# Moving SyncE's DMA transposes behind the output stores, and one spread from GpSimd's queue to SyncE's, in a fused attention and GEGLU kernel

## The chip, the cores and the metric

The kernel runs on one core of a Trainium2 chip. The metric is the device time in microseconds (us), the median of several executions. A second number, the span of a profiled execution, goes from the first to the last instruction of the program in that execution.

Engines are named as the profile names them: PE (TensorE, matmuls; PEld is its weight load), DVE (VectorE), ACT (ScalarE), POOL (GpSimd) and SP (SyncE). SP computes nothing here: it only waits for semaphores and issues DMAs, one after the other, so that an instruction which waits holds up all that stand behind it. A "q" behind an engine's name marks its sequencer.

## The reference

Sliding-window attention with an ALiBi bias over 8 batches of 8 heads, 576 positions and 64 dimensions, then a GEGLU feed-forward block over the 4608 tokens:

```
rel = pos[:, None] - pos[None, :]
mask = (rel >= 0) & (rel < 128)
scores = where(mask, q @ k.T / sqrt(D) + slopes * -abs(rel), -1e9)
attn = softmax(scores) @ v                      # 8 batches, 8 heads, 576 x 64
x = attn.transpose(0, 2, 1, 3).reshape(4608, 512)
g, val = x @ w_gate, x @ w_val                  # 512 -> 1536
out = (gelu(g) * val) @ w_out                   # 1536 -> 512, float32
```

## The kernel before

The feed-forward part runs over nine groups of 512 tokens (`for g in range(NG)`, group 0 to 8). In each group PE first makes the 12 blocks of hidden features (`gate_val` for one block, `gate_quad` for four blocks with seven instead of eight block products), and then the output (`out_products`). Attention for a later batch is woven into the same groups. In groups 2 to 5, group g does this for batch b = g + 2: the scores of b (`scores2`, from the transposed queries `qT` and keys `kT`), the exponentials and the sums over windows (`add`); and for batch b - 1 = g + 1 the row sums (`sums4`), their inverses, the products with the values (`values`) and the scaling into `xT`.

The order on each engine is written by hand: instructions stand on an engine in the order in which the code names them, and semaphores hold each one until what it needs is there. For batches 3 to 7 the data take this way:

- **Loads** on POOL's queue (`load_qk`, `load_v`): at f == 6 of group g POOL issues the q and k rows of batch g + 3 into `qs`, `ks` and the v rows of batch g + 2 into `vb`, 15 DMAs. They follow POOL's own arithmetic of the group.
- **Transposes** on SP's queue (`transposes_dma`): five DMAs turn `qs` into `qT`, one turns `ks` into `kT`. Before the change they are called at the start of groups 1 to 5. For batches 5 to 7 (groups 3 to 5) k comes ahead of q.
- **Gather** on SP's queue (ACT's for batch 3): three small DMAs write the inverse row sums `r` of batch g + 1 to a buffer `rd` in DRAM, issued at f == 5 (for batches 3 and 7 between two steps of the quad at f == 6).
- **Spread** on SP's queue (POOL's for batch 3): two DMAs of 576 KB read `rd` back, each row repeated over 64 partitions, into `rb`, at f == 6. DVE multiplies the value products by `rb` (L554).
- **Stores** on SP's queue: finished output tiles `osb` are collected in a list and issued by `store()`, in the middle of `out_products` and at f == 1 of the next group. The last of a group's tiles is finished by DVE at L927.

In groups 3 to 5 SP's order is therefore: transposes of k, of q, the two stores left from the group before, gather, spread, and two stores in the middle of the products. The first transpose waits for the rows of k, and everything behind it waits with it.

Of the kernel before, what the change touches and what calls it, by code (L numbers as in the profile page):

```python
# [35 lines left out]
def kernel(  # L36
# [10 lines left out]
    nc = tc.nc  # L47
    B, H, S, D = q.shape
# [26 lines left out]
    def keep_busy(ps, n, w=64, rhs=None):  # L75
        for _ in range(n):
# [23 lines left out]
    qs, ks = ([consts.tile([128, 5, DM], BF16, name=f"{nm}s{i}") for i in range(2)]  # L100
              for nm in "qk")
    qT, kT = ([consts.tile([128, 4, 640], BF16, name=f"{nm}T{i}") for i in range(2)]
              for nm in "qk")
# [16 lines left out]
    def load_qk(b):  # L120
        load(qs[b % 2], q, b)
        load(ks[b % 2], k, b)

    def load_v(b, js=range(5)):
        load(vb[b % 2], v, b, js, 64)
# [48 lines left out]
        for n, lo in ((0, 0), (1, 384)):  # L174
            untangle(copy, b, n, what, c, c + 1, ps[:, lo:576])

    def transposes_dma(b):
        def of_k():
            nc.sync.dma_start_transpose(
                out=kT[b % 2].rearrange("p c (j t) -> p (c j) t", t=128),  # L180
                in_=ks[b % 2].rearrange("p j x -> p (j x)"))

        if b > 4:
            of_k()
        for j in range(5):
            nc.sync.dma_start_transpose(
                out=qT[b % 2][:, :, 128 * j:128 * j + 128], in_=qs[b % 2][:, j, :])
        if b <= 4:
            of_k()


    Ps = [consts.tile([128, H, 896], BF16, name=f"P{i}") for i in range(2)]
# [254 lines left out]

    def spread_dma(b):
        for i in (0, 1):
            (nc.gpsimd if b == 3 else nc.sync).dma_start(  # L450
                out=recip[b][64 * i:64 * i + 64, :, :],
                in_=flat[b][i:H:2, :].unsqueeze(0).to_broadcast((64, 4, S)))

# [214 lines left out]
    def store():  # L668
        for args in stores:
            nc.sync.dma_start(**args)  # L670
        stores.clear()
# [79 lines left out]
    def flat_of(t):  # L751
        return t.rearrange("p a x -> p (a x)")
# [10 lines left out]
    def combine_weights(f0, engine=nc.gpsimd):  # L763
        todo, to = [], sums_w[f0]
        for c in (0, 1):
            g1, g2, v1, v2 = (weights(w, x, f0) for w, x in ((wg, c), (wg, 2 + c), (wv, c), (wv, 2 + c)))
            s1, s2, s3, s4 = (cut(t[:, c, :], 2) for t in to)
            todo.append([lambda o=o, a=a, b=b, op=op: engine.tensor_tensor(out=o, in0=a, in1=b, op=op)
                         for o, a, b, op in ((s1, v1, v2, ALU.add), (s2, s1, g1, ALU.subtract),
                                              (s3, g1, v1, ALU.subtract), (s4, g2, s2, ALU.subtract))])  # L770
        return [do for pair in zip(*todo) for do in pair]
# [23 lines left out]
    def tiles_of(ts, lo=0):  # L795
        return [flat_of(t)[:, lo + 512 * i:lo + 512 * i + 512] for t, n in ts for i in range(n)]

    def wide_of(ts):
        return [cut(flat_of(t).bitcast(FP32)[:, 512 * i:512 * i + 512], 2) for t, n in ts for i in range(n)]
# [156 lines left out]
    for h in (0, 2, 4, 6):  # L956
        for w, src in ((0, q), (1, k)):
            (nc.scalar if w and h == 0 else nc.sync).dma_start(  # L958
                out=raw[w][h // 4].rearrange("p (h x) -> p h x", h=4)[:, h % 4:h % 4 + 2, :],
                in_=src[0][h:h + 2, 0:384, :].rearrange("h (p r) d -> p h (r d)", r=3))  # L960
# [114 lines left out]
    for do in inverse_a:  # L1075
        do[1]()
    dve(out=pairs1.rearrange("p x (h d) -> p h x d", d=64),
        in_=vb[1].rearrange("p j x -> p (j x)")[:, 0:1536].rearrange(
            "p (h x d) -> p h x d", h=H, x=3))
# [46 lines left out]
    for n in range(4):  # L1126
        nc.gpsimd.dma_start(
            out=wo[:, 3 * n:3 * n + 3, :],
            in_=moe_w_out[384 * n:384 * n + 384, :].rearrange("(c p) f -> p c f", p=128))
# [193 lines left out]
    put_off = {}  # L1323

    for g in range(NG):
        if 1 <= g < B - 2:
            transposes_dma(3 if g == 1 else g + 2)
        if g == NG - 1:
            nc.gpsimd.tensor_copy(out=mark, in_=flat_of(T)[0:1, 1536:1538])
            sums = combine_weights(4)  # L1330
            for do in sums[:6]:
                do()
            gate_quad(g, 0)
            store()
            for do in sums[6:]:
                do()
            gate_quad(g, 6)
            for lo, hi in ((0, 2), (3, 5)):
                combine_left(g, lo, hi, (0, 1), engine=nc.gpsimd)
            gate_quad(g, 4, (wide_of([(kT[1], 2), (vb[0], 2), (vb[1], 2)]), tiles_of([(qs[1], 4)])), high=nc.vector)  # L1340
            out_products(g)
            continue
        if g == B - 1:
            for f in range(NF):
                if f in QUADS:
                    gate_quad(g, f)
                elif not any(f0 < f < f0 + 4 for f0 in QUADS):
                    gate_val(g, f)
                if f == 4:
                    store()  # L1350
                if f == 5:
                    combine_left(g, 0, 2, (0, 1), engine=nc.gpsimd)
                if f == 6:
                    combine_left(g, 2, 3, (0, 1))
                    combine_left(g, 0, 2, (3, 2), engine=nc.gpsimd)
            for which in ((0, 1), (3,), (2,)):
                for lo, hi in ((3, 5), (5, 6)) if 0 in which else ((2, 5), (5, 6)):
                    combine_left(g, lo, hi, which)
            out_products(g)
            continue  # L1360
        if g == 1:
            room = rooms(1)
            sums = combine_weights(6, nc.vector)
            for do in sums[:5]:
                do()
        for f in range(9 if g == 0 else 0, NF):
            if f == 6 and g:
                gate_quad(g, 6, room if g == 1 else None,
                          (lambda: gather(g + 1)) if g in (2, B - 2) else None)
            elif not (g and 6 < f < 10):  # L1370
                gate_val(g, f)
            if g == 1:
                for do in {0: sums[5:7], 1: sums[7:]}.get(f, ()):
                    do()
                if f in (1, 2, 3):
                    combine_x(1, 0, 256, {1: (0,), 2: (1, 2), 3: (3,)}[f])
                if f in (4, 5, 10, 11):
                    combine_right({4: 0, 5: 1, 10: 2, 11: 3}[f])
            if f in put_off:
                put_off.pop(f)()  # L1380
            if f == 1:
                store()
            if g == 0 and f == 10:
                masks_of_last_blocks(0, 8)
            if g == 0 and f == 9:
                for c in range(4):
                    for w in (0, 1):
                        transpose(1, w, c, (act, dve)[w])
            if g < 2:
                continue  # L1390
            if g == 2 and f == 2:
                add(3, 2, act, (1,))
            if f == (0 if g == 2 else 3 if g == B - 2 else 2):
                nc.gpsimd.tensor_copy(out=mark, in_=hid[g][0:1, f, 510:512])  # L1394
                combine_x(g, engine=nc.gpsimd)
            if f == 3 and 2 < g < B - 2:
                combine_left(g, 0, 2, (0, 1, 3, 2), engine=nc.gpsimd)
            if f == (5 if g == 2 else 4):
                sums4(g + 1)
            if f == 5:  # L1400
                if 2 < g < B - 2:
                    combine_left(g, 2, 3, (0, 1), engine=nc.gpsimd)
                    gather(g + 1)
                else:
                    combine_left(g, 0, 3, (0, 1), engine=nc.gpsimd)
            if g == B - 2 and f == 2:
                combine_x(g + 1, 0, 192)
            if f == 6:
                spread_dma(g + 1)
            if f == 6:  # L1410
                if g + 3 < B:
                    load_qk(g + 3)
                if g + 2 < B:
                    load_v(g + 2)
            if f == 11:
                combine_left(g, 3, 6, (0, 1))
        if g == 1:
            nc.gpsimd.tensor_copy(out=mark, in_=kT[1][0:1, 0, 512:514])
            load_qk(4)
            load_v(3)  # L1420
        if g == 0:
            nc.gpsimd.memset(Ps[0][:, :, 0:64], 0.0)
            for t in (qs[1], ks[1]):
                nc.gpsimd.memset(t[64:128, 4, :], 0.0)
        if g in PRODUCTS:
            out_products(g)
        else:
            for item in steps(g):
                if isinstance(item, int):
                    out_part(g, item)  # L1430
                else:
                    RUN[item[0]](*item[1:])
            store()
        if g == 0:
            load_v(2)
            nc.gpsimd.tensor_copy(out=mark, in_=qT[0][0:1, 0, 512:514])
            load_qk(3)
# [30 lines left out]
```

## Time and profile before

| What | Value |
|---|---|
| Device time, median of 3 executions | 323.19 us (322.78 to 323.5) |
| The profiled execution's own time | 322.87 us |
| Span of that execution | 321.1 us (1.8 us lie around it) |
| Granted TensorE clock, mean | 1.000 |
| Instructions in the span | 9392 |
| Bytes moved by DMA | 43.57 MB, mean 136 GB/s |

The profiled execution is 0.32 us under the median. The page lists the busy time of each engine, the chain of work that ended last, the costliest groups of instructions and the DMA queues. DMA queue q0 carries what POOL issues, q1 what SP and ACT issue, and q8 is a queue of the kind "instruction". The timeline view lists an engine's instructions in order of time, with start and duration in us and, in brackets, the idle time ahead of a row and what ended it. The windows view gives, for a stretch of time, the busy time of each engine and in brackets the number of its instructions that lie in it. The DMA view lists, for a stretch, the packets, megabytes and share of the 16 DMA engines' time of each queue.

### The profile page before, as it was taken

The page shows a single profiled execution, that of the slowest core. Times are in us where ns is not written, and L with a number is a line of the kernel's source. Part 1 is how long each engine was busy: PE and PEld are TensorE (multiplying, and loading weights), DVE is VectorE, ACT ScalarE, POOL GpSimd, SP SyncE. Part 2 cuts the span into 40 slices and gives each one's busy share as a digit, 9 for nine tenths or more (in the row PEclk, how much of TensorE's full clock was granted, in tenths as well). Part 3 has the DMA queues.
Part 4 walks back from the last instruction along what each step waited for, and adds up shares of the span by engine and source line. Part 5 has one row for each costly group of instructions (what it writes and reads, how often), then busy time and mean ns, then how long its engine had stood idle before and what let it go on. Part 6 is the DMA issues. An engine that isn't in the chain of part 4 may idle for free.

```text
span 321.1 us, 9392 instructions
## 1 busy us (share of the span) xinstructions
PE 314.4 (98%) x3729; PEld 214.9 (67%) x3729; DVE 251.5 (78%) x493; ACT 222.3 (69%) x427; POOL 207.1 (65%) x239
## 2 busy tenths in 40 slices
PE   8999999999999999999999999999999999999995
PEld 3566746465554768476765786578747787788884
DVE  7789666979779887978698679877898856895883
ACT  7984678557888688757865787578767256627852
POOL 5974579384068977589856995496009496446750
PEclk9999999999999999999999999999999999999999
DMA  8999999999999959994999499949203330003003
GB/s 213 168 195 192 199 178 184 141 172 193 95 181 165 153 128 208 171 145 133 188 193 153 141 187 195 150 138 179 101 34 83 72 133 0 0 2 133 0 4 131
DMA packets 149724, 43.57 MB, mean 136 GB/s; under 512 B 133688, under 2 KB 143024, under 8 KB 149680
## 3 DMA queue, kind: packets, MB, share of 16 engines
q0 software_dynamic: 107744, 19.28, 76.6%
q1 hardware_dynamic: 41472, 23.35, 32.5%
q8 instruction: 29, 0.48, 0.6%
q10 hardware_dynamic: 464, 0.35, 0.3%
q14 instruction: 15, 0.12, 0.2%
HBM read 43.65 MB, written 9.53 MB: 166 GB/s over the span
## 4 chain that ended last, share of the span: by engine, by line
PE 94%; DMA 2%; DVE 1%; issue 1%; ACT 1%; SPq 1%; DVEq 0%
PE ps L644 35%; PE ps L837 21%; PE ps L748 21%; PE ps L495 6%; PE ps L680 4%; PE ps L306 2%; PE ps L700 2%; PE ps L220 2%; DMA ks<-in_k_dram 2%; PE ps L434 1%; PE ps L158 1%; SPq L958 1%; ACT P L235 0%; DVE xT L534 0%; ACT rb L597 0%
## 5 line engine op out<-in xcount | busy, mean ns | idle before, releaser
L644 PE MATMUL ps<-xT,wv 128*128 128x512 bf16 (+3 forms) x292 | 67.7, 353 | 0.0
L644 PE MATMUL ps<-xT,wg 128*128 128x512 bf16 (+3 forms) x292 | 67.6, 353 | 0.0
L650 ACT ACTIVATE gelu<-ps 128x512 bf16<-128x512 f32 (+3 forms) x73 | 39.3, 544 | 37.7 <-PE ps L644 33.9
L235 ACT ACTIVATE P<-ps 128x512 bf16<-128x512 f32 (+1 forms) x108 | 52.3, 578 | 5.2 <-PE ps L306 3.3
L651 DVE TENSOR_TENSOR hT<-ps,gelu 128x512 bf16<-128x512 f32 (+3 forms) x73 | 43.3, 619 | 15.3 <-PE ps L644 12.0
L644 PEld LDWEIGHTS <-wv 128*128 128x128 bf16 x292 | 27.5, 98 | 28.3 <-issue 0.2
L644 PEld LDWEIGHTS <-wg 128*128 128x128 bf16 x292 | 26.8, 98 | 25.2 <-issue 1.0
L116 POOL DMA_DIRECT2D vb<-in_v_dram x40 | 34.1, 880 | 6.9 <-DMA ks<-in_k_dram 2.0
L240 DVE TENSOR_TENSOR P<-P,emask 128x768 bf16<-128x768 bf16 x60 | 31.9, 554 | 7.6 <-ACT P L235 5.7
L748 PEld LDWEIGHTS <-hT 128*128 128x128 bf16 x336 | 32.0, 98 | 5.6
L116 POOL DMA_DIRECT2D ks<-in_k_dram x30 | 25.4, 887 | 3.3 <-DMA rb<-rd 2.0
L837 PEld LDWEIGHTS <-kept 128*128 128x128 bf16 x256 | 25.0, 98 | 3.0
L748 PEld LDWEIGHTS <-left 128*128 128x128 bf16 x252 | 24.2, 98 | 4.2 <-issue 0.9
L116 POOL DMA_DIRECT2D qs<-in_q_dram x30 | 25.4, 869 | 1.8 <-DMA wo<-in_moe_w_out_dram 1.0
L1394 POOL COPY mark<-hT 1x2 bf16<-1x2 bf16 x5 | 0.9, 174 | 35.1 <-DVE hT L651 35.1
L748 PE MATMUL ps<-right,hT 128*128 128x256 bf16 x168 | 22.2, 273 | 0.0
L845 DVE TENSOR_TENSOR qT<-ps,qT 128x512 f32<-128x512 f32 x20 | 12.9, 686 | 11.2 <-PE ps L837 9.8
L748 PE MATMUL ps<-right,left 128*128 128x256 bf16 x168 | 20.6, 273 | 0.8 <-issue 0.8
L748 PE MATMUL ps<-wo,hT 128*128 128x256 bf16 x168 | 21.2, 273 | 0.0
L837 PE MATMUL ps<-xT,wg 128*128 128x256 bf16 x176 | 21.0, 273 | 0.0
L845 DVE TENSOR_TENSOR P<-ps,P 128x512 f32<-128x512 f32 x24 | 15.0, 682 | 6.9 <-PE ps L837 6.9
L837 PEld LDWEIGHTS <-wg 128*128 128x128 bf16 x176 | 17.2, 98 | 3.4 <-issue 0.2
(179 smaller groups left out, 639.1 us busy)
## 6 DMA issues: line engine op xcount, KB each, us to landing
out_dram<-osb SPq DMA_DIRECT2D x34, 256.0 KB
rb<-rd SPq DMA_DIRECT2D x8, 576.0 KB
vb<-in_v_dram POOLq DMA_DIRECT2D x32, 128.0 KB, 6.8
qs<-in_q_dram POOLq DMA_DIRECT2D x24, 128.0 KB, 6.5
ks<-in_k_dram POOLq DMA_DIRECT2D x24, 128.0 KB, 7.8
wo<-in_moe_w_out_dram POOLq DMA_DIRECT2D x4, 384.0 KB, 12.1
wg<-in_moe_w_gate_dram POOLq DMA_DIRECT2D x5, 256.0 KB, 8.2
wv<-in_moe_w_val_dram POOLq DMA_DIRECT2D x5, 256.0 KB, 8.8
```

The source lines that it names most:

```text
L116: nc.gpsimd.dma_start(out=t[at:at + n, j, :].rearrange("p (h d) -> p h d", h=H), in_=src[b][:, 128 * j:128 * j + n, :].rearrange("h p d -> ...
L220: nc.tensor.matmul(out=out, lhsT=keys(b, c, m)[half, :], rhs=qT[b % 2][half, c, q0:q0 + n], start=first, stop=True, skip_group_check=not f ...
L235: nc.scalar.activation(out=dst, in_=src, func=AF.Exp, scale=0.125)
L240: nc.vector.tensor_tensor(out=dst, in0=dst, in1=m, op=ALU.mult)
L495: mm = nc.tensor.matmul(out=out, lhsT=lhsT, rhs=prob(b)[half, c, i, col:col + q1 - q0], start=all(t[2] != u for t in todo[:n]), stop=True, ...
L644: nc.tensor.matmul(out=ps, lhsT=w[:, c, 128 * f:128 * (f + 1)], rhs=xT[:, c, t0 + lo:t0 + hi], start=begins, stop=(c == 3), skip_group_che ...
L650: nc.scalar.activation(out=gl[:, 0:n], in_=pg, func=AF.Gelu)
L651: nc.vector.tensor_tensor(out=hid[g][:, f, lo:hi], in0=pv, in1=gl[:, 0:n], op=ALU.mult)
L680: nc.tensor.matmul(out=acc[g], lhsT=hid[g][:, f, 128 * t:128 * (t + 1)], rhs=wo[:, f, :], start=(f == 0), stop=(f == NF - 1))
L748: nc.tensor.matmul(out=made[g, a, into], lhsT=lhsT, rhs=rhs, start=first and k == 0, stop=count + k == NF // 2 - 1, skip_group_check=True)
L837: nc.tensor.matmul(out=ps[:, 256 * e:256 * e + 256], lhsT=lhsT, rhs=x[:, c, :], start=n in (1, 2, 5) and e == 0 and c == 0, stop=c == 1, s ...
L845: nc.vector.tensor_tensor(out=to[u], in0=cut(banks[n, u], to[u].shape[1]), in1=to[u], op=ALU.add)
```

## The change

The transposes of groups 1 and 2 stay where they were, at the start of the group. Those of groups 3 to 5 move to f == 1, behind `store()`, and q comes ahead of k in all of them. The spread of batch 3 is issued by SP instead of POOL.

```diff
-    def transposes_dma(b):
-        def of_k():
-            nc.sync.dma_start_transpose(
-                out=kT[b % 2].rearrange("p c (j t) -> p (c j) t", t=128),
-                in_=ks[b % 2].rearrange("p j x -> p (j x)"))
-
-        if b > 4:
-            of_k()
-        for j in range(5):
-            nc.sync.dma_start_transpose(
-                out=qT[b % 2][:, :, 128 * j:128 * j + 128], in_=qs[b % 2][:, j, :])
-        if b <= 4:
-            of_k()
+    def transposes_dma(b, what=range(6)):
+        for j in what:
+            if j == 5:
+                nc.sync.dma_start_transpose(
+                    out=kT[b % 2].rearrange("p c (j t) -> p (c j) t", t=128),
+                    in_=ks[b % 2].rearrange("p j x -> p (j x)"))
+            else:
+                nc.sync.dma_start_transpose(
+                    out=qT[b % 2][:, :, 128 * j:128 * j + 128], in_=qs[b % 2][:, j, :])
...
     def spread_dma(b):
         for i in (0, 1):
-            (nc.gpsimd if b == 3 else nc.sync).dma_start(
+            nc.sync.dma_start(
...
     for g in range(NG):
-        if 1 <= g < B - 2:
-            transposes_dma(3 if g == 1 else g + 2)
+        if 1 <= g < 3:
+            transposes_dma(g + 2)
...
             if f == 1:
                 store()
+                if 2 < g < B - 2:
+                    transposes_dma(g + 2)
...
             if f == 6:
                 spread_dma(g + 1)
-            if f == 6:
                 if g + 3 < B:
                     load_qk(g + 3)
```

SP's instructions from the transposes of group 2 to the middle of group 3, in the kernel before (numbers in the names are buffers; L670 stores, L186 and L179 transposes, L445 gather, L450 spread):

```order
L186 DMA_TRANSPOSE qT_99<-qs_95 128x4x128 x5
L179 DMA_TRANSPOSE kT_101<-ks_97 128x20x128
L670 DMA out_dram<-osb 128x512 x2
L179 DMA_TRANSPOSE kT_102<-ks_98 128x20x128
L186 DMA_TRANSPOSE qT_100<-qs_96 128x4x128 x5
L670 DMA out_dram<-osb 128x512 x2
L445 DMA rd<-r 8x192 x3
L450 DMA rb<-rd 64x4x576 x2
```

The same stretch in the changed kernel, whose lines are four fewer (L666 stores, L184 and L180 transposes, L441 gather, L446 spread):

```order
L184 DMA_TRANSPOSE qT_99<-qs_95 128x4x128 x5
L180 DMA_TRANSPOSE kT_101<-ks_97 128x20x128
L446 DMA rb<-rd 64x4x576 x2
L666 DMA out_dram<-osb 128x512 x4
L184 DMA_TRANSPOSE qT_100<-qs_96 128x4x128 x5
L180 DMA_TRANSPOSE kT_102<-ks_98 128x20x128
L441 DMA rd<-r 8x192 x3
L446 DMA rb<-rd 64x4x576 x2
```

The spread of batch 3 now stands behind the transposes of batch 4; the two stores of the middle of group 2 and the two left over stand together as four; q and k have changed places. In groups 4 and 5 the order changes in the same way. On POOL, the end of group 2 before the change:

```order
L721 TENSOR_TENSOR left<-left,hT 128x768
L892 TENSOR_TENSOR hT<-P_105,vb_103 128x2x256 x2
L450 DMA rb<-rd 64x4x576 x2
L116 DMA qs_96<-in_q_dram 128x8x64 x4
L116 DMA qs_96<-in_q_dram 64x8x64
L116 DMA ks_98<-in_k_dram 128x8x64 x4
```

and in the changed kernel:

```order
L717 TENSOR_TENSOR left<-left,hT 128x768
L888 TENSOR_TENSOR hT<-P_105,vb_103 128x2x256 x2
L116 DMA qs_96<-in_q_dram 128x8x64 x4
L116 DMA qs_96<-in_q_dram 64x8x64
L116 DMA ks_98<-in_k_dram 128x8x64 x4
```

The two DMAs of the spread are gone from POOL, and the loads of batch 5 follow its last multiplication directly. PE, DVE and ACT keep their instructions in the same order.

## The prediction

> **What bounds the kernel now.** I read the page first, then PE group by group, then its one gap.
>
> ```profile
> PE 314.4 (98%) x3729; PEld 214.9 (67%) x3729; DVE 251.5 (78%) x493; ACT 222.3 (69%) x427; POOL 207.1 (65%) x239
> PE 94%; DMA 2%; DVE 1%; issue 1%; ACT 1%; SPq 1%; DVEq 0%
> q8 instruction: 29, 0.48, 0.6%
> ```
>
> PE is busy for 98% of the span and makes 94% of the chain that ended last. SP and POOL, on which everything in this change stands, are nearly absent from the chain. So the change can only pay, or cost, where PE waits. The windows of groups 2, 3, 4 and 5, cut where PE begins each group's first gate product, show how much that is (columns: length, busy PE, PEld, DVE, ACT, POOL, clock, DMA share, GB/s):
>
> ```profile
> 95.67:128.96 33.29, 33.29 (x410) 22.99 (x405) 28.76 (x53) 26.74 (x48) 28.37 (x32) 1.00 1.60 166
> 128.96:163.16 34.20, 33.44 (x406) 23.04 (x404) 27.30 (x56) 24.82 (x43) 26.74 (x30) 1.00 1.40 165
> 163.16:196.44 33.28, 33.28 (x406) 23.04 (x404) 26.84 (x56) 24.72 (x43) 27.03 (x31) 1.00 1.41 168
> 196.44:229.72 33.28, 33.28 (x406) 23.04 (x404) 26.86 (x55) 24.71 (x43) 17.58 (x19) 1.00 1.11 149
> ```
>
> Three groups take 33.28 or 33.29 us without an idle moment. Group 3 takes 34.20: 0.92 more for the same instructions. That is all that this stretch can give. PE's timeline shows where it lies:
>
> ```profile
> 151.00 0.87 PE L306 MATMUL ps<-qT,kT 64*64 64x64 bf16 x44
> 157.31 0.38 PE L748 MATMUL ps<-right,left 128*128 128x256 bf16 x2
> 158.45 1.25 PE L748 MATMUL ps<-right,left 128*128 128x256 bf16 x10 [0.76 <-issue]
> ```
>
> At 157.69 PE stops in the middle of a product and stands for 0.76 us (0.92 with the refilling), though it waits for no engine and no data: "issue". I look for it in queue q8. Its 29 packets for 7458 matmuls and weight loads are one per 257: each brings a block of about 256 PE instructions, and PE stops if the next block is late. Windows from the start count the instructions up to a time, and the DMA view shows when the packet came:
>
> ```profile
> 0.00:151.03 151.03, 148.74 (x1881) 90.64 (x1881) 120.33 (x236) 112.00 (x222) 104.61 (x132) 1.00 1.55 168
> 0.00:157.69 157.69, 155.40 (x2009) 96.33 (x2010) 125.37 (x246) 117.86 (x235) 111.09 (x139) 1.00 1.54 170
> q1 hardware_dynamic: 494, 1.10, 98.4%
> q8 instruction: 1, 0.02, 6.2%
> ```
>
> Up to 157.69 PE has 4019 instructions, up to 151.03 it has 3762: one block, begun as the scores begin. The third row is the whole stretch from 151.03 to 155.69, in which q1 fills the DMA engines to 98.4% and no q8 packet starts; the fourth is 155.69 to 157.02, the packet at last: 6.2% of 16 engines over 1.33 us, so 1.32 us long. PE goes on 1.43 us after its end. If the block is asked for as the one before is entered, it waited 4.66 us behind those 1.10 MB on q1. They are the spread of batch 4, issued by SP at 149.59 (below).
>
> [...]
>
> **The change, part by part.** SP's timeline from the transposes of group 2 on, then the rows of other engines that release it:
>
> ```profile
> 96.11 7.85 SPq L186 DMA_TRANSPOSE qT<-qs  x5
> 107.23 6.20 SPq L179 DMA_TRANSPOSE kT<-ks  x1
> 123.20 0.81 SPq L670 DMA_DIRECT2D out_dram<-osb  x2
> 134.73 4.04 SPq L179 DMA_TRANSPOSE kT<-ks  x1
> 138.82 6.51 SPq L186 DMA_TRANSPOSE qT<-qs  x5
> 145.44 1.00 SPq L670 DMA_DIRECT2D out_dram<-osb  x2
> 146.53 1.93 SPq L445 DMA_DIRECT2D rd<-r  x3
> 149.59 1.33 SPq L450 DMA_DIRECT2D rb<-rd  x2
> 127.38 3.12 DVE L554 TENSOR_TENSOR xT<-ps,rb 128x320 bf16<-128x320 f32 x10
> 131.71 0.42 DVE L927 TENSOR_TENSOR osb<-ps,osb 128x256 f32<-128x256 f32 x1
> 138.81 1.35 DVE L437 RECIPROCAL r<-ps 128x192 f32<-128x192 f32 x1
> ```
>
> *Group 3, the term that counts.* Before, SP stands from 124.01 to 134.73, until the rows of k have landed, and the finished stores stand behind it. Now the stores go when DVE has finished the last tile, at 132.13, and end 1.00 later, at 133.2. Then come five transposes of q, one of k, the gather (its input is there at 140.16, earlier than SP), 1.13 us from the gather's end to the spread (148.46 to 149.59), and some 0.1 between. q costs 6.51 without loads beside it and 7.85 with them (group 2); I take 7.0, since the loads run into the first of the five. k costs 4.04 alone and 6.20 under loads; I take 4.1, since it comes last. The spread is issued at 133.2 + 7.0 + 4.1 + 1.9 + 1.1 + 0.1 = 147.4, **2.2 us earlier** than 149.59. With both small costs it is 146.9, 2.7 earlier; with both large ones 150.4, 0.8 later.
>
> The packet for PE's block moves with the spread's end: from 155.69 to 153.5, done at 154.8, PE could go on at 156.2, and asks for it at 157.69. The gap goes: **-0.92 us**. 0.9 of the 2.2 would do.
>
> *q ahead of k, and k last.* k's transpose ends at about 144.4 on SP, where before q's ended at 145.33. The scores begin at 151.00, so there is cover of over 6 us either way: 0. Beyond it, each us late would be a us of PE.
>
> *Groups 4 and 5.* The same order, the same sums from their rows:
>
> ```profile
> 165.88 0.42 DVE L927 TENSOR_TENSOR osb<-ps,osb 128x256 f32<-128x256 f32 x1
> 181.78 1.30 SPq L450 DMA_DIRECT2D rb<-rd  x2
> 199.19 0.42 DVE L927 TENSOR_TENSOR osb<-ps,osb 128x256 f32<-128x256 f32 x1
> 213.86 1.30 SPq L450 DMA_DIRECT2D rb<-rd  x2
> 194.86 3.12 DVE L554 TENSOR_TENSOR xT<-ps,rb 128x192 bf16<-128x192 f32 x10
> ```
>
> From L927's end to the spread it is again 1.0 + 7.0 + 4.1 + 1.9 + 1.1 + 0.1 = 15.2: 181.5 and 214.8, so 0.3 earlier and 0.9 later. PE has no gap in either group, and `rb` is first used at 194.86 in group 4, 12 us after its issue, and in group 5 one group length (33.28) after that: 0.
>
> *The spread of batch 3 on SP.* POOL's timeline in group 2, and ACT's last gather:
>
> ```profile
> 111.69 1.15 ACTq L445 DMA_DIRECT2D rd<-r  x2
> 116.90 1.32 POOL L450 DMA_DIRECT2D rb<-rd  x2
> 118.19 4.27 POOL L116 DMA_DIRECT2D qs<-in_q_dram  x5
> 126.23 2.44 POOL L116 DMA_DIRECT2D ks<-in_k_dram  x3 [2.03 <-DMA rb<-rd]
> 130.83 3.32 POOL L116 DMA_DIRECT2D vb<-in_v_dram  x4 [1.28 <-DMA qs<-in_q_dram]
> ```
>
> SP is free at 113.43, behind the transpose of k; the gather is in at 112.84 + 1.13 = 114.0. So SP issues the spread at 114.0, where POOL came to it at 116.90. POOL loses 1.32 us of issue and the wait of 2.03, so the loads of batch 5 run 1.3 to 3 us earlier. DVE first needs `rb` at 127.38. Nothing of this reaches PE: 0; it only makes the loads' overlap with group 3's transposes smaller. If SP were late here instead, L554 would take it up from 127.38 on, and PE after it.
>
> *Sum.* 322.87 - 0.92 = 321.95 for the profiled execution. It lay 0.32 under the median of 323.19, so I expect 322.27 as a median, and say **322.3**.
>
> **The rivals.** *The gap stays or only moves (323.2).* For it: the fetch is my reading of one packet, and the three times shown differ by 0.72, almost the gap, so the median execution may hold other gaps. Against it: the 98.4% row. Time: no change. [...]
>
> *Another block gives it back (322.4 to 323.2).* The block after next ends at 195.46:
>
> ```profile
> 0.00:190.52 190.52, 187.47 (x2392) 118.30 (x2395) 151.35 (x299) 141.37 (x275) 135.52 (x167) 1.00 1.52 170
> 0.00:195.46 195.46, 192.41 (x2520) 122.61 (x2521) 155.10 (x308) 145.96 (x283) 140.46 (x173) 1.00 1.53 171
> q0 software_dynamic: 3158, 0.40, 241.9%
> q8 instruction: 1, 0.02, 6.0%
> ```
>
> Again 254 instructions lie between. From 190.52 to 193.1 the loads on q0 hold the engines; the packet starts at 193.1 and takes 6.0% of 16 engines over 1.0 us, 0.96. It ends 1.40 ahead of 195.46, where 1.43 was needed above: just in time. Each tenth that the loads of group 4 delay it further is a tenth of idle PE, and the earlier spread shifts those loads by about 0.3. A delay of 0.1 to 0.9 gives 322.4 to 323.2.
>
> *The transposes run slow under the loads (324.0, slower).* If q costs 7.85 and k 6.20, as in group 2, group 3's spread comes 0.8 later, its packet too, and the gap grows from 0.92 to 1.7: 323.19 + 0.8 = 324.0. It decides from a spread issued at 150.2 on. Against it: POOL has issued the last load at 134.15 even before the change, and 1.3 to 3 us earlier after it, while k is issued only at 140.2.
>
> **How the numbers follow.** Forecast 0.57, no change 0.25, given back 0.10, slow transposes 0.08. A measurement tells about 0.2% (0.65 us) from no change. The forecast lies 0.89 below the median, so I leave 0.10 of its 0.57 within 0.2%; that and the first two rivals make 0.45. Faster: 0.47, slower: 0.08. The range leaves out the slow case, reaches up to no change with the 0.2 by which runs above it may lie, 323.4, and down to 321.8, the profiled sum with 0.15 for executions better than it.
>
> **What would show it.** Right: group 3 as long as group 4 (33.3), no gap near 157.7, the spread at about 147.4, q8's packet at least 1.4 us plus its length ahead of PE's stop. Wrong: a gap of the same size with the spread earlier (then it isn't the fetch behind the spread), a new "issue" gap near 195, or transposes of q above 8 us.

## The result and the profile after

| | Before | After |
|---|---|---|
| Median | 323.77 us (322.78 to 327.03, 20 executions) | 322.00 us (321.34 to 322.96, 20 executions) |
| Profiled execution | 322.87 us, span 321.1 | 322.07 us, span 320.3 |

The ratio is 0.9945, 95% interval 0.9929 to 0.9962: about 1.8 us faster by the ratio. Between the two profiled executions the difference is 0.80 us. The windows of groups 2 to 5 of the changed kernel, cut as before (length, then busy time of PE, PEld, DVE, ACT and POOL):

```profile
95.90:129.19 33.29, 33.29 (x410) 22.95 (x405) 28.68 (x53) 26.74 (x48) 29.17 (x32) 1.00 1.67 168
129.19:162.48 33.29, 33.29 (x407) 23.02 (x404) 26.86 (x56) 24.72 (x43) 27.00 (x31) 1.00 1.53 174
162.48:195.76 33.28, 33.28 (x406) 23.02 (x404) 26.84 (x56) 24.72 (x43) 25.26 (x30) 1.00 1.35 164
195.76:229.03 33.27, 33.27 (x406) 23.01 (x404) 26.84 (x55) 24.72 (x43) 17.60 (x20) 1.00 1.09 147
```

Group 3 is now as long as its neighbours: 33.29 where it was 34.20. SP's timeline of groups 3 to 5, stores, transposes, gather and spread (the line numbers are four lower):

```profile
123.44 9.27 SPq L666 DMA_DIRECT2D out_dram<-osb  x4
132.82 7.46 SPq L184 DMA_TRANSPOSE qT<-qs  x5
140.51 3.29 SPq L180 DMA_TRANSPOSE kT<-ks  x1
143.90 1.93 SPq L441 DMA_DIRECT2D rd<-r  x3
147.06 1.30 SPq L446 DMA_DIRECT2D rb<-rd  x2
...
173.50 3.04 SPq L180 DMA_TRANSPOSE kT<-ks  x1
...
179.72 1.75 SPq L446 DMA_DIRECT2D rb<-rd  x2
...
212.27 1.30 SPq L446 DMA_DIRECT2D rb<-rd  x2
```

The spread of batch 4 stands at 147.06 instead of 149.59. PE's timeline at the place of the old gap:

```profile
157.55 1.47 PE L744 MATMUL ps<-right,left 128*128 128x256 bf16 x12
```

Before, PE stopped behind the second of these products of `right` and `left`; now all twelve run without a break. The DMA view shows the packet for PE's block, first the stretch from 151.27, in which none comes, then 153.75 to 155.06:

```profile
q1 hardware_dynamic: 247, 0.54, 101.3%
...
q8 instruction: 1, 0.02, 6.2%
```

The packet still waits behind q1, but behind 0.54 MB instead of 1.10, and it is there 2.71 us before PE starts the third product at 157.77. So the wait, which ended in time, cost nothing here: PE is busy for all of group 3's 33.29 us.

### The profile page after: what moved, and what is told of

It is laid out like the page before. It is cut to its first block, busy times and chain, and to the rows that moved or that the text cites. A ratio compares the mean times of both kernels' runs of the same rounds, so it can differ in the third digit from the quotient of the medians.

```text
span 320.3 us, 9400 instructions
## 1 busy us (share of the span) xinstructions
PE 314.1 (98%) x3729; PEld 214.8 (67%) x3729; DVE 251.5 (79%) x493; ACT 222.2 (69%) x427; POOL 206.0 (64%) x237
## 4 chain that ended last, share of the span: by engine, by line
PE 93%; ACT 2%; DMA 1%; DVE 1%; issue 1%; SPq 0%; DVEq 0%
PE ps L640 34%; PE ps L833 21%; PE ps L744 21%; PE ps L491 5%; PE ps L676 4%; PE ps L302 2%; PE ps L696 2%; PE ps L216 1%; DMA qs<-in_q_dram 1%; ACT P L231 1%; PE ps L430 1%; PE ps L158 1%; SPq L954 0%; DVE xT L530 0%; ACT L646 0%
```

## The experiments

Two theories stand against each other. The **fetch theory**, that of the prediction: PE stops because the packet with its next 257 or so instructions (one packet for 257 in the profile of before) waits behind the spread, so the spread's time sets the gap. The **rival**: the gap only moves, or comes from something else that the change touched (order of the transposes, the spread of batch 3). Each ratio is against the kernel before on the same chip, in the same series. A profile shows one execution of a kernel, often one of its faster ones.

### The parts, one at a time

Only the spread of batch 3 from POOL to SP, in the kernel before:

```diff
-            (nc.gpsimd if b == 3 else nc.sync).dma_start(
+            nc.sync.dma_start(
                 out=recip[b][64 * i:64 * i + 64, :, :],
```

> The kernel before with one part of the change: batch 3's spread on SP, the transposes where they were. Fetch theory (PE loses time because its next instruction block waits behind the spread of batch 4): the loads of batch 5 land about 1.1 us earlier (as in the changed kernel), SP's k transpose in group 3, which waits for them, starts at about 133.6 instead of 134.7, and the spread of batch 4 is issued at about 148.5. The gap near 157.7 shrinks by 1.1 us: none in a profile like that of before, and about 1.0 us off the median. Rival (the loads on POOL's queue are what matters, not the transposes): the whole gain of 1.8 us. Rival (only the order on SP's queue matters): no change, gap of about 0.8 us.

Measured: 323.39 us against 323.92, ratio 0.9969 (0.994 to 0.9999). SP and PE in its timelines:

```profile
133.55 4.03 SPq L179 DMA_TRANSPOSE kT<-ks  x1
...
148.51 1.32 SPq L450 DMA_DIRECT2D rb<-rd  x2
```
```profile
158.00 1.25 PE L748 MATMUL ps<-right,left 128*128 128x256 bf16 x10 [0.48 <-issue]
```

k's transpose starts at 133.55 instead of 134.73, and so the spread of batch 4 comes 1.08 earlier; the gap shrinks from 0.76 to 0.48, and does not go as expected: counted from the start of group 3, the packet ends only 0.45 earlier (27.61 for 28.06). The prediction put this part at nothing; while the transposes stand where they stood, it is worth something.

Only the transposes, that is the changed kernel with batch 3's spread put back on POOL:

```diff
-            nc.sync.dma_start(
+            (nc.gpsimd if b == 3 else nc.sync).dma_start(
                 out=recip[b][64 * i:64 * i + 64, :, :],
```

> The changed kernel, but batch 3's spread stays on POOL: only the transposes of groups 3 to 5 behind the stores, q ahead of k. Fetch theory: the spread of batch 4 no longer hangs on the landing of k's rows but on DVE's last output tile; issued at 147 to 148, no gap near 157.7, group 3 as long as group 4 (33.3 us), the whole gain of about 1.8 us in the median. Rival (loads on POOL's queue matter): no gain, or the smaller part of it.

Measured: 322.49 us, ratio 0.9952 (0.9928 to 0.9977); spread at 147.02, no gap:

```profile
147.02 1.33 SPq L446 DMA_DIRECT2D rb<-rd  x2
```
```profile
157.01 1.47 PE L744 MATMUL ps<-right,left 128*128 128x256 bf16 x12
```

The transposes carry the gain. What the spread of batch 3 adds on top (0.9945 against 0.9952) is inside the intervals.

Only the order, q ahead of k, at the old place at the start of the group:

```diff
-        if b > 4:
-            of_k()
         for j in range(5):
...
-        if b <= 4:
-            of_k()
+        of_k()
```

> The kernel before with q ahead of k in groups 3 to 5, at the old place at the start of the group, ahead of the stores; spread of batch 3 on POOL. Fetch theory: SP starts with q when its rows have landed, near 130.4, is through with k at about 142, and issues the spread of batch 4 at 146 to 147: no gap near 157.7 and the gain of about 1.8 us, although nothing is moved behind the stores. Rival (the stores had to go first): the gap stays, no gain.

Measured: 323.14 us, ratio 0.9967 (0.9943 to 0.9991). SP and PE:

```profile
127.20 7.08 SPq L184 DMA_TRANSPOSE qT<-qs  x5
139.14 4.97 SPq L179 DMA_TRANSPOSE kT<-ks  x1
...
148.38 1.33 SPq L447 DMA_DIRECT2D rb<-rd  x2
```
```profile
157.83 1.25 PE L745 MATMUL ps<-right,left 128*128 128x256 bf16 x10 [0.26 <-issue]
```

q now uses the time in which SP stood, 127.20 to 134.3, but it runs beside the loads of k: the last rows of k land at 139.00 here, at 134.58 in the kernel before. So k starts 4.4 later, and the spread is only 1.2 earlier, not the 2.6 to 3.6 expected (148.38 for 146 to 147).

Only the place: behind the stores, but k ahead of q as before.

```diff
-        for j in what:
+        for j in ((5, 0, 1, 2, 3, 4) if b > 4 else what):
```

> The changed kernel with only the order turned back: k ahead of q in groups 3 to 5, both still behind the stores. If the place behind the stores is what counts, k takes 4.0 and q 6.5 us, the spread comes at about 147 and there is no gap: same as the change (322.0). If the order counts as well, because k is the one that suffers from the loads that still run at 132.8 (6.20 us under loads in group 2), the spread comes at 148.5 to 149, the packet for PE's block at about 155, and 0.2 to 0.5 us of the gap come back: 322.3 to 322.6.

Measured: 323.59 us against 324.07, ratio 0.9989 (0.9956 to 1.0022): no gain that shows. SP and PE:

```profile
134.11 4.83 SPq L180 DMA_TRANSPOSE kT<-ks  x1
138.99 6.50 SPq L184 DMA_TRANSPOSE qT<-qs  x5
...
148.74 1.31 SPq L446 DMA_DIRECT2D rb<-rd  x2
```
```profile
157.86 1.25 PE L744 MATMUL ps<-right,left 128*128 128x256 bf16 x10 [0.56 <-issue]
...
195.66 0.49 PE L744 MATMUL ps<-right,hT 128*128 128x256 bf16 x3 [0.62 <-issue]
```

Against the change, counted from the start of group 3 (128.57 here, 129.19 there), the spread is 2.30 later: the transposes start 1.91 later (k's rows land at 133.97, and the last store is issued by 132.10), at the end of the loads k takes 1.54 more than it took behind q in the change, q takes 0.96 less, and 0.19 less lies between the steps. So **both are needed** to close the gap in the profiles: the place behind the stores lets q run when the rows of k are nearly in, and q, which waits for nothing, fills the time until k can go. By the medians the order alone gains something too (0.9967), and the intervals don't tell how much of the change's gain that is. A second gap, at 195.66, costs this execution another 0.78 (group 4 took 34.06).

### Holding the spread alone

The cleanest test is the changed kernel with nothing else moved but the spread of batch 4, by idle DMAs in front of it on SP. Four into one buffer:

```diff
     def spread_dma(b):
+        if b == 4:
+            idle = d_pool.tile([H, S], FP32, name="idle")
+            for _ in range(4):
+                nc.sync.dma_start(out=idle[:, 0:192], in_=sumrow[b][0:128:16, 0:192])
```

> The changed kernel with four small idle DMAs (6 KB each, to a scratch buffer, about 0.65 us of SP each) ahead of the spread of batch 4, so that it goes 2.6 us later, near 149.7, about where it was before the change. Fetch theory: in the five profiles so far the block's packet starts 6.1 to 6.7 us after the spread's issue; it comes near 156.1, ends near 157.3, PE goes on near 158.7 and stands for about 0.9 us near 157.8: 0.5 to 1.2 us slower than the changed kernel (ratio to before about 0.997). Rival (what the change gained lies elsewhere on the queues: stores, transposes, loads): no gap, as fast as the changed kernel (ratio about 0.9945).

Measured: 325.57 us, ratio 1.0038 (1.0005 to 1.0071). SP and PE:

```profile
148.18 5.47 SPq L448 DMA_DIRECT2D idle<-r  x4
153.82 1.31 SPq L450 DMA_DIRECT2D rb<-rd  x2
```
```profile
152.41 0.81 PE L302 MATMUL ps<-qT,kT 64*64 64x64 bf16 x32
155.25 0.42 PE L302 MATMUL ps<-qT,kT 64*64 64x64 bf16 x12 [2.03 <-SPq L209]
```

The idle DMAs, which write one buffer, waited for each other (5.47 us of SP for the four; with a buffer each, below, 2.31), and the spread was issued after PE had begun the scores, at 152.41, where by the reading above it asks for its block. The packet then went ahead of the spread (153.22 to 154.51), 0.81 behind the start of the scores, and the gap at the third product did not come. PE stood elsewhere: at SP itself. In `scores2` one half of the scores may only write its bank once the other half is done, and that is passed on by `relay`, an empty instruction on SP's queue. It stands behind the spread, so an SP that is still held when the first half is done (at 152.41 + 0.81) stops PE directly. (Another 0.99 of this execution, a wait for k's transpose at 93.16 in group 1, lies ahead of the idle DMAs.) Nine idle DMAs show the same, larger:

```diff
-            for _ in range(4):
+            for _ in range(9):
```

> The same with nine idle DMAs: the spread of batch 4 goes 5.8 us later, near 152.9, after the block has been asked for (near 151.2). Fetch theory: the packet goes ahead of the spread, before 153, and there is no gap near 157.8, although the spread is later than in any run so far; as fast as the changed kernel within 0.3 us unless the late spread makes DVE's scaling at about 161.5 wait. Rival (a late spread as such costs PE time): a gap of 2 us or more, slower than before.

Measured: 341.05 us, the median of three executions, ratio 1.0542 (1.0484 to 1.06); a fourth took 649.36 us, for a reason that nothing here shows. In the profile SP is held for 20.74 us, and PE stands 17.06 at the relay:

```profile
169.58 0.64 PE L302 MATMUL ps<-qT,kT 64*64 64x64 bf16 x12 [17.06 <-SPq L209]
```

The expected time was missed, since the relay was not thought of, but the part on the packet came true. It starts at 152.42, 0.71 behind the start of the scores (151.71), where it started 4.66 behind in the kernel before. From the start of the scores to the packet, q1 moved 0.01 MB here and 1.10 MB there. Without the spread in front of it the packet came 0.71 us behind the start of the scores and not 4.66, so in the kernel before it is the spread that it waited for. To avoid the chain, four idle DMAs each with a buffer of its own:

```diff
-            idle = d_pool.tile([H, S], FP32, name="idle")
-            for _ in range(4):
-                nc.sync.dma_start(out=idle[:, 0:192], in_=sumrow[b][0:128:16, 0:192])
+            idle = [d_pool.tile([H, S], FP32, name=f"idle{i}") for i in range(4)]
+            for i in range(4):
+                nc.sync.dma_start(out=idle[i][:, 0:192], in_=sumrow[b][0:128:16, 0:192])
```

> The changed kernel with four idle DMAs in front of batch 4's spread on SP, each into a buffer of its own in DRAM, so that none waits for another (one kernel before held the spread to 153.82, by a chain, and PE then stood at the relay on SP's queue and not at a block). At about 0.65 us each they put the spread at 149.7 instead of 147.06, where it stood before the change, and its queue ends at about 151.0, ahead of the relay at about 152.4. Fetch theory: the packet for PE's block comes at about 155.7 instead of 153.75, PE stands for 0.5 to 0.9 us at about 157.8, group 3 takes 33.8 to 34.2 and the execution about 322.7. Rival (the gap has another cause than the spread's place, for example the order of q and k): no gap at 157.8, group 3 stays at 33.3.

Measured: 322.62 us, ratio 0.9961 (0.9939 to 0.9984). The hold missed its size: SP waits some 1.1 us for the gather in any case, and about half of the idle DMAs' 2.31 lay in that wait; besides, q and k took 0.52 less than in the change.

```profile
144.91 2.31 SPq L448 DMA_DIRECT2D idle<-r  x4
147.39 1.30 SPq L450 DMA_DIRECT2D rb<-rd  x2
```
```profile
157.10 1.50 PE L748 MATMUL ps<-right,left 128*128 128x256 bf16 x12
```

The spread is 0.77 later than in the change, counted from the group's start, and the packet ends at 155.91, 1.29 later. PE begins the third product at 157.34, 1.43 behind the packet's end, which is the least in the table below, and group 3 takes 33.29. So the expected gap did not come, and the packet was just early enough. This is the fastest of the ten executions (321.76); whether others, slower by up to 1.88, had the gap is not shown. Three idle DMAs more were to bring the spread to its old place:

```diff
-            idle = [d_pool.tile([H, S], FP32, name=f"idle{i}") for i in range(4)]
-            for i in range(4):
+            idle = [d_pool.tile([H, S], FP32, name=f"idle{i}") for i in range(7)]
+            for i in range(7):
```

> The changed kernel with seven idle DMAs in front of batch 4's spread, three more than in the kernel whose spread came at 147.39, 18.64 us after the start of group 3: those four lay almost wholly in the 1.1 us that SP waits for the gather anyway. Three more of 0.58 us put the spread 20.4 us behind the start of group 3; before the change it was 20.6 (149.59 - 128.96), and its two DMAs end 21.7 behind it, ahead of the relay at about 23. Order and place of the transposes stay as in the change, so only the spread's time is that of before. Fetch theory: the packet for PE's block ends about 27.8 behind the group's start, PE goes on 1.4 later where it would want to at 28.6: a gap of 0.4 to 0.8 at the place of the gap of before, group 3 takes 33.8 to 34.1, the execution about 322.7. Rival (q and k's place or order acts on the gap in another way than by the spread's time): no gap, group 3 at 33.3, 322.0.

Measured: 323.26 us against 324.40, ratio 0.9976 (0.9952 to 1.0001), beside 322.00 for the change. The profiled execution, with 324.33 one of the longest of its ten, doesn't show the case it was made for: q took 8.58 in it, the spread came at 151.28, and PE stood at the relay.

```profile
153.48 0.42 PE L302 MATMUL ps<-qT,kT 64*64 64x64 bf16 x12 [1.70 <-SPq L209]
```

By the medians the change loses by the hold, but the two intervals overlap (up to 0.9962 for the change), and how much of it is the block and how much the relay in the other nine executions stays open. So no run has the spread alone at its old place with the gap back; that the spread's time sets the gap rests on the packet in the two kernels with the chain and on the table below.

### Moving the block's boundary

If the gap belongs to a boundary between blocks, more instructions at PE's start must move it. The warm-up's seven matmuls of 512 columns, cut into 56 of 64, add 98 PE instructions to the kernel before:

```diff
-    keep_busy(held[0], 7, 512, zeros[:, 0:1].to_broadcast((128, 512)))
+    keep_busy(held[0], 56, 64, zeros[:, 0:1].to_broadcast((128, 512)))
```

> The kernel before, its DMAs and their order untouched; the seven warm-up matmuls of 512 columns at the start of PE become 56 of 64 columns, while PE waits for the first loads anyway. That is 98 more PE instructions, so each block of 256 begins 98 instructions earlier in the work. Fetch theory: the block that began at 151.0 in group 3 now begins near 141, ahead of the spread, and the next one near 154: no gap at 157.7, group 3 takes 33.3 to 33.5 us, 0.5 to 1.8 us off the median unless another block now falls behind a spread. Rival (the gap belongs to that product, its data or SP's order, not to the fetch): gap of 0.8 us or more at the same product, no gain.

Measured: 325.36 us, ratio 1.0036 (1.0011 to 1.0061). The gap at 157.7 is gone, though SP's order is that of before; instead there is a new one, larger, in group 2, and a small one further on in group 3, which takes 33.80. PE's timeline, and the DMA view from 123.00 to 126.86 and from there to 127.84:

```profile
129.23 0.25 PE L495 MATMUL ps<-P,vb 64*64 64x64 bf16 x4 [1.56 <-issue]
...
162.72 0.56 PE L495 MATMUL ps<-P,vb 64*64 64x192 bf16 x25 [0.28 <-issue]
```
```profile
q0 software_dynamic: 4315, 0.58, 225.9%
...
q8 instruction: 1, 0.02, 6.2%
```

Here the packet comes late while POOL's loads on q0 hold the engines, and PE goes on 1.39 behind its end (1.49 at the small gap). The gap follows the boundary; the time that was expected to be gained was lost at another block.

The same in the changed kernel, with a shift chosen from its trace so that no short block would fall behind the loads:

```diff
-    keep_busy(held[0], 7, 512, zeros[:, 0:1].to_broadcast((128, 512)))
+    keep_busy(held[0], 103, 35, zeros[:, 0:1].to_broadcast((128, 512)))
```

> The changed kernel with the seven warm-up matmuls of 512 columns cut into 103 of 35, so that PE's blocks of 256 instructions begin 192 instructions earlier in the work. Counted in the trace of the changed kernel this puts the shortest block but the first at 4.8 us (at 12.3) where now some take 4.5 (at 11.0 and 222.8) and 4.9 (189.8, behind the loads), and none of the boundaries then falls shortly behind a spread or the loads. Fetch theory: fewer late blocks, the 0.25 us at 15.94 may go, and the other executions lose less: 321.4 to 321.9 if it works, and no gap over 0.3 anywhere. Rivals: the short matmuls make the warm-up longer than 3.6 us, or a late block appears at another place, as in the kernel before with a shift of 98: 322.3 to 324.

Measured: 323.24 us, ratio 0.9972 (0.9942 to 1.0002), no faster than the change. A gap of 0.37 stands in the opening (0.25 in the change), and groups 3 to 5 are as good as in the change (33.29, 33.28, 33.27). The 0.40 by which the profiled execution (322.47) is longer than that of the change lie in group 2, 33.70 for 33.29, most of it where PE waits at 117.40 for DVE and not for a packet. Five of its twelve executions lie at 323.88 or above, four of them with a granted clock of 0.993; what does that was not found. No version beats the change.

### The kernel before, twice more

> The kernel before, once more, for its profile: its times scatter from 322.6 to 328.1, those of the changed kernel from 321.3 to 323.0. Fetch theory: the spread of batch 4 hangs on the landing of k's rows in the kernel before and scatters with it; the gap near 157.7 is (issue of the spread + 6.4 + 1.2 + 1.4) less the time when PE asks, about 157.5, and other gaps of the kind issue follow late packets of q8. Rival: gaps of the same size every time, and the scatter lies elsewhere.

> The kernel before, a second sample for its profile. Fetch theory and rival as for before_again_1: the gap near 157.7 follows the spread's issue by the same sum, and further idle time of the kind issue, if any, follows late packets of q8.

They took 324.07 and 323.40 us. Windows of groups 3 and 4, and PE's timeline, of the first:

```profile
129.71:163.20 33.49, 33.44 (x406) 23.04 (x404) 26.97 (x56) 24.72 (x43) 25.31 (x29) 1.00 1.36 161
163.20:197.65 34.45, 33.44 (x406) 23.01 (x404) 28.00 (x59) 24.72 (x43) 27.85 (x31) 1.00 1.37 164
```
```profile
196.67 0.49 PE L748 MATMUL ps<-right,hT 128*128 128x256 bf16 x3 [1.01 <-issue]
```

and of the second:

```profile
128.94:163.32 34.38, 33.44 (x406) 23.02 (x404) 27.18 (x56) 24.83 (x43) 26.02 (x30) 1.00 1.40 165
163.32:197.00 33.68, 33.45 (x407) 23.03 (x405) 27.23 (x57) 24.72 (x43) 28.15 (x32) 1.00 1.39 164
```
```profile
158.62 1.25 PE L748 MATMUL ps<-right,left 128*128 128x256 bf16 x10 [0.94 <-issue]
...
196.02 0.49 PE L748 MATMUL ps<-right,hT 128*128 128x256 bf16 x3 [0.23 <-issue]
```

The kernel before loses time at one or the other of two blocks, or at both: 0.91, 1.37 and 1.49 us in groups 3 and 4 together, against 66.57 in the change. The block at 196 is the one that the prediction had found just in time.

### One block, nine executions

Everything about the block of group 3, put side by side. Spread and packet are in us behind the start of group 3; "PE behind packet" is from the packet's end to the third product of `right` and `left`; "excess" is group 3's length above 33.29.

| Execution | Spread issued | Packet ends | PE behind packet | Excess |
|---|---|---|---|---|
| before, second again | 20.58 | 28.23 | 1.45 | 1.09 |
| before | 20.63 | 28.06 | 1.43 | 0.91 |
| k ahead of q, behind the stores | 20.17 | 27.87 | 1.43 | 0.71 |
| only batch 3's spread | 19.73 | 27.61 | 1.61 | 0.64 |
| only the order | 19.54 | 27.50 | 1.49 | 0.41 |
| changed, four idle DMAs apart | 18.64 | 27.16 | 1.43 | 0.00 |
| only the transposes | 18.36 | 25.90 | 2.67 | 0.00 |
| after | 17.87 | 25.87 | 2.71 | 0.00 |
| before, first again | 20.91 | 27.06 | 1.72 | 0.20 |

In the eight upper rows, whatever was edited and differences under 0.2 aside, an earlier spread means an earlier packet and a smaller excess, until the packet is early enough and the excess is nothing. In this table PE never goes on less than 1.43 us behind its packet. The last row is off the line: its spread is the latest and its packet comes early. Held further still, to 22.36 in the profile of the seven idle DMAs, the spread lets the packet pass ahead of it altogether (its end is 24.03 behind the start), as in the two kernels with the chain. So the harm seems to be done by a spread issued shortly before PE asks, not by a late one as such.

## Why the prediction was right, point by point

**PE's stop is a late block.** Right, and shown: it moves with the boundary, its length follows the packet, and PE goes on 1.4 to 1.7 us behind the packet's end at every gap of the table. Not every packet costs a stop: beside 29 packets, the waits of PE that the profile of before lists have one on "issue", the 0.76 us of this gap, and those of the profile after have one, 0.25 us in the opening. In six of the nine rows the packet of the table was late, for 0.20 to 1.09 us.

**The spread 2.2 us earlier, at 147.4.** Right for the changed kernel: 147.06, 2.53 earlier. q took 7.46 (7.0 assumed) and k 3.29 (4.1). The packet was expected from 153.5 to 154.8 and came from 153.75 to 155.06. The gap of 0.92 went, and the profiled execution came out at 322.07 for 321.95. That the spread came so near to 147.4 is in part luck, since errors of the sum offset each other: the stores ended 0.36 behind DVE's last tile (132.35 to 132.71) where 1.00 was put, q took 0.46 more, k 0.81 less, and the steps lay 0.47 further apart.

**"q ahead of k, and k last: 0" was argued from the wrong user.** The prediction asked only whether the scores would get k in time. The order matters for the spread, which stands behind both: with k first the same move gains nothing that shows (0.9989). The sum was right because it put q first, at 133.2, with its rows in, and k last and short. The gain that the text gave to the place behind the stores is that of place and order together.

**Groups 4 and 5: a worth of 0 was too little, and 214.8 was wrong.** The spreads came at 179.72 and 212.27, where 181.5 and 214.8 were expected, 2.1 and 1.6 earlier than before and not 0.3 earlier and 0.9 later. Of the 1.8 and 2.5 by which the forecast missed, 0.68 is the earlier start of both groups, which the prediction had not carried on, 1.0 is k, taken at 4.1, which took 3.04 and 3.06 behind q, and 0.6 the stores, which ended 0.36 behind DVE's last tile and not 1.00. PE has no gap in these groups of the profiled execution, so that execution says 0. But in two others of the kernel before, group 4 lost 1.17 and 0.40 us to its own block, which in the profile of the change was ready 2.18 us ahead. The rival "another block gives it back" had the sign reversed: the change took delay away from that block too. That the earlier spread did it was not tried by itself.

**The size: -0.89 was forecast from the median shown, 1.8 was measured.** The mis-sized term is the only one in the sum, 0.92, read from one execution of the kernel before that happened to be a good one: 322.87, where the median of 20 is 323.77. The two executions of before profiled later account for their longer times within 0.05: the first is 1.20 longer than the execution of the prediction, 0.46 of it in groups 3 and 4 and 0.75 ahead of group 2 (which starts at 96.42 instead of 95.67); the second is 0.53 longer, with 0.58 more in groups 3 and 4. What makes the longest executions of before, up to 327.03, is not shown. That 322.3 came near the 322.00 measured is in part luck: the median of three from which it set out was 0.58 too low, and the gain 0.88 too small.

**The spread of batch 3 at 114.0: 0.** It was issued at 115.81, since the gather, put at 1.13, was in only 2.73 behind its last issue on ACT (113.08). The loads of batch 5 began at 117.13, 1.06 earlier, the near end of the 1.3 to 3 given being missed. In the change its worth can't be told from 0, as forecast; alone it shortens the gap by 0.28, by the way through k's rows.

**Slow transposes under the loads** did not happen in the profile of the change. They did in three executions of the changed kernel with idle DMAs, ahead of these: q took 8.12 and 8.20 in group 3 of the two with the chain and 8.58 in that with seven. The price that the prediction gave was the later packet; it left out that SP's queue also carries the relay, which stopped PE for 1.70 us in the last of them.

## What to carry to other kernels

A PE gap that ends on "issue" between two instructions with no dependence is worth a look at the instruction queue. At every such gap of the table a packet ended 1.43 to 1.72 us before PE went on, and here the gap closed when the spread, whose 1.10 MB had been moved ahead of the packet while PE's block ran, was issued 2.53 us earlier. On SP's queue it paid to put q first, whose data were in, and to keep k's DMA, which waited for loads, behind it: neither the new place (a gap of 0.56 left) nor the new order (0.26) closed the gap without the other. Where such gaps come and go, as the 0.91, 1.37 and 1.49 us of the three profiles of the kernel before do, read more than one execution before pricing their removal.

## What the runs showed of the hardware

- q8 brought 29 packets of 0.48 MB together beside PE's 7458 instructions, one for 257, in the profile of before. A packet took 0.88 to 1.33 us there and 0.89 to 2.02 us in the profile after; the one of the table took 1.33 us before, 1.31 us after and 1.21 us with the four idle DMAs apart. Where PE had to wait for one, it went on 1.34 us (at 17.18, in the opening of the last block shift) to 1.72 us (the first repeat of before) behind its end.
- The packet of the table came late in the kernel before while q1 held the engines (98.4% in the 4.66 us ahead of it), the one of the first block shift while q0 did (225.9% in the 3.86 us shown, with no packet).
- In the execution in which PE stood for 17.06 us, q8 brought a packet at 152.42 and the next one at 178.50.
- k's single transpose took 3.00 to 4.38 us last behind q in groups 3 to 5 where both stood behind the stores, 4.83 with its rows only 0.14 us in and the last loads still running, and 5.73 in group 2 of the change under loads. In return, where q was transposed beside the loads, the last rows of k landed 4.4 us later (139.00 for 134.58).
- In the execution in which PE stood for 17.06 us, from 152.52 on, the granted clock was 0.50 from 155.1 to 175.5, and the twelve products of `right` and `left` behind the stop took 2.74 us for 1.47. The mean clock of that execution was 0.970; the other profiled executions had 0.999 or 1.000.
